# Heads 0 to 3 in the lower partitions, 4 to 7 in the upper: other pieces for the loads of a recurrence ahead of two matmul layers

## The chip, the cores and the metric

The kernel runs on one core of a Trainium2 chip. The metric is the device time of one execution in microseconds (us). PE is TensorE's matmul side, DVE is VectorE, ACT is ScalarE, POOL is GpSimd; SP issues nearly all DMA transfers of this kernel, in program order, from one queue.

## The reference, cut to what matters

```python
# attention: batch 4, heads 8, sequence 768, head size 48, fp32
for t in range(S):
    cur = einsum('bhd,bhe->bhde', u * k[t], v[t])
    y[t] = einsum('bhd,bhde->bhe', r[t], state + cur)
    state = w * state + einsum('bhd,bhe->bhde', k[t], v[t])
x = y.transpose(0, 2, 1, 3).reshape(3072, 384)
h = maximum(maximum(x @ w1, x @ w2), x @ w3); x = h @ w_out     # 384 -> 768 -> 384
g = x @ w_gate; out = (silu(g) * (x @ w_val)) @ w_out2          # 384 -> 1536 -> 384
```

## The kernel before, in words

**Units and chunks.** The sequence is cut into NB = 6 chunks of T = 128 steps. A unit is one chunk of one batch, so there are 24 units, numbered n = 4 i + b. For each unit the recurrence is done as matmuls: scores of keys against queries, masked and with a bonus on the diagonal, and a state of 48x48 per head carried from chunk to chunk. Units 0 to 3 (no state yet) are done whole at the start. From unit 4 on a unit is done in halves of 64 steps (`half`, planned as `h n`): `h n` holds the scores and state sums of unit n and the outputs y of unit n - 1.

**What a unit loads.** `load_columns` (L304, tile `qk`) brings r and reversed k with head dimension on partitions: 112 partitions by 4096 bytes that lie together, one transfer of 448 KB. `load_sides` (L325, tile `nat`, planned as `rows`) brings k, v and r with time on partitions, half the heads beside the other half, in four transfers of 144 KB. Before the change, x, the half of the partitions, holds the even or the odd heads, so that a piece of a row that lies together in memory is one head: 48 floats, 192 bytes.

**What is done with them.** DVE scales the columns by the powers of w (`prep_scores`, L342, planned as `scaled`). POOL prepares the rows (L355, L356, L360). DVE masks the scores (L405), adds up states (L515, L521) and reduces the bonus (L375). ACT copies the outputs y from PSUM into `xr` with two copies (`evacuate`, L476, planned as `row`).

**The layers between.** After a chunk's four units, two transfers (`repack`, L526, xr<-xr) bring the chunk to 128 partitions, and the first layer runs on 512 tokens: `m` (up projections, three matmul products for each pair of high and low words), a maximum over three branches on DVE (L568), its split (L580 on ACT, L583 on DVE) and `o`. Chunk 0 runs without a repack. All of this is interleaved with the units of the next chunks. The second layer (`g`, `oo`) follows from about 320 us on and has TensorE to itself.

**The weights** come in 64-bit form in 42 pieces, k = 0 to 41 (`fetch`, L226, tile `raw`, three buffers). Each is put together by ACT (L235, L242), DVE (`top` L275 and `rest` L281), ACT (L286) and POOL or DVE (`lo`, L289).

**Order.** TensorE's order is written out by hand (`order` and `slots`: `h 4` to `h 8` stand among the `m` of chunk 0). The order of the other engines and of SP's queue comes from `Plan`, a list scheduler with a cost and an earliest time for each step. Every engine runs its list in order, and so does SP: an issue that waits for a buffer holds up all later issues. `branch` (L768) tests once for decays outside a range, and what stands behind it in a list is issued after it.

Of the kernel before, what the change touches and what calls it, by code (L numbers as in the profile page):

```python
# [21 lines left out]
T = 128  # L22
# [161 lines left out]
def rwkv_moe(ctx: ExitStack, tc: tile.TileContext, qk, nat, kn, vn, rn, wcol, wh, uh, wup1, wout1, wup2, out):  # L184
# [116 lines left out]
    def load_columns(n):  # L301
        a = (h_tile([112, 2, NPAIR, T], f"qk_{n}") if n in (2, 3)
             else atp.tile([112, 2, NPAIR, T], F32, tag="qk", name=f"qk_{n}"))
        nc.sync.dma_start(out=a, in_=qk[n].rearrange("p (q j t) -> p q j t", q=2, j=NPAIR))  # L304
        inp[n] = [a]
# [9 lines left out]
    def load_sides(n):  # L315


        shape, name = [128, 2, 3, NPAIR, D], f"nat_{n}"
        if n == B:
            late["nat"] = wpool.tile([128, 2, *shape[1:]], F32, tag="w", name="nat_4_5")  # L320
        t = (late["nat"][:, n - B] if n < B + 2 else xpool.tile(shape, F32, tag=f"x2_{NB - 1}", name=name) if n == 2 * B
             else atp.tile(shape, F32, tag="nat", name=name))
        for x in range(2):
            for g in range(2):
                nc.sync.dma_start(out=t[64 * x:64 * x + 64, g].rearrange("p q j d -> p (q j) d"),  # L325
                                  in_=nat[n, 64 * g:64 * g + 64].rearrange("p (z x d) -> p x z d", x=2, d=D)[:, x])
        kvr[n] = [t[:, :, q] for q in range(3)]
        flats[n] = t.rearrange("p g q j d -> p (g q j d)")
# [4 lines left out]
    def prep_scores(n):  # L333
        a = inp[n][0]
        if n < B:
            nc.vector.tensor_tensor(out=a, in0=a, in1=powers.unsqueeze(1).to_broadcast([112, 2, NPAIR, T]), op=ALU.mult)
        else:

            halved = powers.rearrange("p j (e t) -> p j e t", e=2)[:, :, ::-1]
# [73 lines left out]
    def apply(n):  # L413
# [9 lines left out]
        for j, x, r in heads:  # L423
            h = 2 * j + x
            nc.tensor.matmul(y[r:r + D, j], v[:, h * D:(h + 1) * D], am[:, x, j], start=True, stop=True)

    def half_scores(n):
        return sc[n][:, 0].rearrange("p j (e t) -> p j e t", e=2)
# [4 lines left out]
    def half(n, before):  # L433


        works, others = [], []
        if n is not None:
            a, k, v = inp[n][0], flats[n], kvr[n][1]
            sc[n] = ps_s.tile([128, 2, NPAIR, T], F32, tag="s", name=f"s_{n}")
            for e in range(1 if n >= (NB - 1) * B else 2):  # L440
                for j in range(NPAIR):
                    for x in range(2):
                        r, c, m = 64 * x, ((1 - e) * 3 * NPAIR + j) * D, wide(x)
                        works.append((half_sums(n)[r:r + m, e, j], k[r:r + 64, c:c + m], v[r:r + 64, 1 - e, j], {}))
            for e in range(2):
                for j in range(NPAIR):
                    for x in range(2):
                        r, g = 64 * x, 64 * (1 - e)
                        works.append((half_scores(n)[r:r + 64, j, e], a[r:r + D, 1, j, g:g + 64], a[r:r + D, 0, j, 64 * e:64 * e + 64], {}))
        if before is not None:  # L450
            a, v, am = inp.pop(before)[0], kvr.pop(before)[1], ams[before]
            y = ys[before] = ps_y.tile([128, NPAIR, 2, T // 2], F32, tag="y", name=f"y_{before}")
            for e in range(2):
                s = (mids[before] if e else states[before]).rearrange("p (j d) -> p j d", j=NPAIR)
                for j in range(NPAIR):
                    for x in range(2):
                        r, to = 64 * x, y[64 - 64 * x:64 - 64 * x + D, j, e]
                        others.append((to, s[r:r + D, j], a[r:r + D, 0, j, 64 * e:64 * e + 64],
                                       dict(start=not e and not j, stop=False, skip_group_check=True)))
# [29 lines left out]
    def outer(n):  # L489
        ku, v = inp.pop(n)[1]  # L490
        ups[n] = ps_m.tile([128, NPAIR, D], F32, tag="m", name=f"u_{n}")
        kf = ku.rearrange("p h d -> p (h d)")
        for j in range(NPAIR):
            for x in range(2):
                r, h, m = 64 * x, 2 * j + x, wide(x)
                nc.tensor.matmul(ups[n][r:r + m, j], kf[:, h * D:h * D + m], v[:, h], start=True, stop=True)

# [7 lines left out]
    def decay(n, eng):  # L505
        s, m = (t.rearrange("p (j d) -> p j d", j=NPAIR) for t in (states[n], mids[n]))
        if eng is nc.scalar:
            for j in range(NPAIR):
                eng.mul(m[:, j], s[:, j], w128[0:112, j:j + 1])
            return  # L510
        eng.tensor_tensor(out=m, in0=s, in1=w128[0:112].unsqueeze(2).to_broadcast([112, NPAIR, D]), op=ALU.mult)

# [113 lines left out]
    with tc.manual_schedule():  # L626
# [49 lines left out]

        P = raw_p.tile([128, HALF], F32, tag="t", name="P")[:, 0:NPAIR * T].rearrange("p (j t) -> p j t", j=NPAIR)
        PT = tab.tile([128, H, D], F32, name="PT")
# [24 lines left out]
        square(6)  # L703
        w128 = pw[:, 7]

# [23 lines left out]
        def power_keys(eng):  # L729
            eng.tensor_tensor(  # L730
                out=P, in0=P, in1=pw[:, 6].unsqueeze(2).to_broadcast([128, NPAIR, T]), op=ALU.mult)

        def turn(_):
            pt_ps = late["pt"] = ps_y.tile([128, NPAIR, 2, 64], F32, tag="y", name="pt_ps")
            for j in range(NPAIR):
                nc.tensor.transpose(pt_ps[:, j].rearrange("p a d -> p (a d)"), P[:, j], ident)

# [95 lines left out]

        plan = Plan(dict(pe=6.4, dve=5.7, act=6.5, pool=3.3, sync=21.5, none=0.0), order)
        add = plan.add
# [73 lines left out]
        for n in range(B, NB * B):  # L909
            i, last = n // B, n >= (NB - 1) * B  # L910

            done = [("h", n - 1)] if n > B + 1 else []
            add(("load", n), {"sync": 1.3}, done or [("s", n - B)], lambda e, n=n: load_columns(n), lag=2.5,
                at=0.0 if done else 17.0 + 2 * n - 2 * B)
            space = [("rows", B)] if n == B + 1 else [("u", n - B - 2)] if n in (B + 2, B + 3) else [("h", n - 2 if n < 11 else n - 1)] if n > 2 * B else []
            if n > B:
                add(("rows", n), {"sync": 3.6}, space, lambda e, n=n: load_sides(n), lag=2.5, at=17.0 if n < 2 * B else 40.0)
# [3 lines left out]
            add(("scaled", n), {"dve": 1.35}, [("load", n), ("low", B - 1), ("lo", 1)], lambda e, n=n: prep_scores(n))  # L921
            add(("keys", n), {"pool": 1.03}, [("bonus", n), ("sided",)], lambda e, n=n: prep_keys(n))
# [12 lines left out]
            add(("row", n), {"act": 1.17}, [("h", n + 1)] + ([("xlo", i - 1, k) for k in range(NK)] if i > 1 else []),  # L935
                lambda e, n=n: evacuate(n))
# [162 lines left out]
```

## Time and profile before

| | |
|---|---|
| median of 3 runs | 832.49 us (832.34 to 834.37) |
| the profiled execution | 831.82 us, span 830.1 us |
| TensorE busy | 814.2 us (98% of the span), mean granted clock 0.995 |
| VectorE, ScalarE, GpSimd busy | 366.1, 302.9, 137.1 us |
| DMA | 83065 packets, 73.78 MB, 66520 of the packets under 512 bytes |

The span runs from the first instruction to the last; the 1.7 us between it and the execution's time lie around it. The engines' shares are averages over stages that differ: units 0 to 3 up to about 26 us, then chunk 0 of the first layer with `h 4` to `h 8` up to about 100 us, then a long stretch up to 320 us, then the second layer.

### The profile page before, as it was taken

Reading aid. Unit: us, or ns where it says so; the run is one execution under the profiler, and the core shown is the slowest. Engines: PE = TensorE matmul, PEld = TensorE weight load, DVE = VectorE, ACT = ScalarE, POOL = GpSimd, SP = SyncE. Lnnn points to the kernel's source line nnn. Section 1 sums busy time; section 2 is a strip of 40 time slices with the busy share of each in tenths; the row PEclk is TensorE's granted clock in tenths of the full one; section 3 lists DMA queues with packets and bytes.
Section 4 is the critical chain, followed back from the end, with each engine's and each line's share of the span. In section 5 each row is a group of like instructions: output and inputs, shape, how many; then the busy total and the mean of one; then the engine's idle time right before and its main releaser. Section 6 shows DMA issues by size and latency. Waiting matters only on the chain.

```text
span 830.1 us, 14338 instructions
## 1 busy us (share of the span) xinstructions
PE 814.2 (98%) x6058; PEld 672.0 (81%) x6058; DVE 366.1 (44%) x554; ACT 302.9 (36%) x579; POOL 137.1 (17%) x147
## 2 busy tenths in 40 slices
PE   9978899999999999999999999999999999999998
PEld 8766688888888888888888888888888888888886
DVE  7779866637565644234663222322222222223222
ACT  5577763425444422224672211312221122123211
POOL 5653525233342320000120000000000000000000
PEclk9989999999999999999999999999999999999999
DMA  9896954675767464311230100100010010001001
GB/s 254 200 215 175 255 131 139 145 203 142 168 198 166 112 204 177 110 65 58 87 113 1 39 0 1 39 0 1 1 39 0 1 39 0 1 1 39 0 1 38
DMA packets 83065, 73.78 MB, mean 89 GB/s; under 512 B 66520, under 2 KB 67544, under 8 KB 82232
## 3 DMA queue, kind: packets, MB, share of 16 engines
q1 hardware_dynamic: 82992, 72.86, 32.4%
q8 instruction: 47, 0.77, 0.4%
q14 instruction: 18, 0.15, 0.1%
q10 hardware_dynamic: 8, 0.00, 0.0%
HBM read 57.51 MB, written 14.16 MB: 86 GB/s over the span
## 4 chain that ended last, share of the span: by engine, by line
PE 90%; DMA 3%; DVE 2%; ACT 1%; issue 1%; SPq 0%; DVEq 0%; ACTq 0%
PE g L549 12%; PE g L551 12%; PE g L550 12%; PE m L549 8%; PE m L551 8%; PE m L550 8%; PE oo L549 6%; PE oo L551 6%; PE oo L550 6%; PE o L549 3%; PE o L550 3%; PE o L551 3%; PE s L467 2%; DMA qk<-in_qk 2%; PE y L467 2%
## 5 line engine op out<-in xcount | busy, mean ns | idle before, releaser
L549 PE MATMUL g<-xhi,w_c 128*128 128x512 f32 x432 | 168.0, 389 | 0.0
L550 PE MATMUL g<-xlo,w_c 128*128 128x512 f32 x432 | 168.0, 389 | 0.0
L551 PE MATMUL g<-xhi,w_c 128*128 128x512 f32 x432 | 168.0, 389 | 0.0
L606 DVE TENSOR_TENSOR g<-mm,g 128x512 f32<-128x512 f32 x72 | 50.1, 696 | 257.0 <-PE g L551 256.3
L549 PE MATMUL m<-xhi,w_a 128*128 128x512 f32 x324 | 129.1, 398 | 1.9 <-ACT am L384 1.7
L551 PE MATMUL m<-xhi,w_a 128*128 128x512 f32 x324 | 127.4, 393 | 2.7 <-DVE w_a L289 2.6
L550 PE MATMUL m<-xlo,w_a 128*128 128x512 f32 x324 | 127.1, 392 | 1.1 <-DVE xlo L544 0.9
L602 ACT ACTIVATE mm<-g 128x512 f32<-128x512 f32 x72 | 43.1, 599 | 151.0 <-PE g L551 151.0
L551 PEld LDWEIGHTS g<-xhi,w_c 128*128 128x128 f32 x432 | 81.1, 188 | 16.9
L550 PEld LDWEIGHTS g<-xlo,w_c 128*128 128x128 f32 x432 | 81.1, 188 | 16.8
L549 PEld LDWEIGHTS g<-xhi,w_c 128*128 128x128 f32 x432 | 81.1, 188 | 16.7
L611 ACT CAST gs<-g 128x512 fp32r<-128x512 f32 x72 | 42.3, 587 | 134.5 <-DVE g L606 134.5
L549 PE MATMUL oo<-gs,w_c 128*128 128x512 f32 x216 | 84.0, 389 | 0.0
L550 PE MATMUL oo<-gs,w_c 128*128 128x512 f32 x216 | 84.0, 389 | 0.0
L551 PE MATMUL oo<-gs,w_c 128*128 128x512 f32 x216 | 84.0, 389 | 0.0
L551 PEld LDWEIGHTS m<-xhi,w_a 128*128 128x128 f32 x324 | 61.2, 189 | 16.6 <-DVE w_a L289 3.8
L549 PEld LDWEIGHTS m<-xhi,w_a 128*128 128x128 f32 x324 | 61.1, 189 | 16.2 <-ACT am L384 1.8
L550 PEld LDWEIGHTS m<-xlo,w_a 128*128 128x128 f32 x324 | 61.1, 189 | 14.3 <-DVE xlo L544 1.8
L583 DVE TENSOR_TENSOR gs<-g,gs 128x512 fp32r<-128x512 f32 x72 | 49.8, 691 | 43.2 <-ACT gs L611 43.2
L580 ACT CAST hs<-m 128x512 fp32r<-128x512 f32 x33 | 19.3, 586 | 81.6 <-DVE m L568 81.4
L551 PEld LDWEIGHTS oo<-gs,w_c 128*128 128x128 f32 x216 | 40.6, 188 | 8.4
L550 PEld LDWEIGHTS oo<-gs,w_c 128*128 128x128 f32 x216 | 40.6, 188 | 8.4
(131 smaller groups left out, 1141.8 us busy)
## 6 DMA issues: line engine op xcount, KB each, us to landing
raw<-in_wup SPq DMA_DIRECT2D x36, 576.0 KB, 6.0
nat<-in_nat SPq DMA_DIRECT2D x80, 144.0 KB, 4.7
qk<-in_qk SPq DMA_DIRECT2D x24, 448.0 KB, 5.2
aside<-parts SPq DMA_DIRECT2D x12, 576.0 KB, 5.4
w_c<-aside SPq DMA_DIRECT2D x6, 1152.0 KB, 5.3
out<-ob SPq DMA_DIRECT2D x18, 256.0 KB, 2.1
raw<-in_wout SPq DMA_DIRECT2D x6, 384.0 KB, 4.2
y<-x SPq DMA_DIRECT2D x3, 768.0 KB, 8.3
```

The source lines that it names most:

```text
L467: nc.tensor.matmul(to, w, x, **(how or dict(start=True, stop=True)))
L549: nc.tensor.matmul(p, wh_, xh, start=first, stop=False)
L550: nc.tensor.matmul(p, wh_, xl, start=False, stop=False)
L551: nc.tensor.matmul(p, wl_, xh, start=False, stop=last)
L580: nc.scalar.copy(hsplit[i, f][0], banks["m", i, f, 2])
L583: nc.vector.tensor_tensor(out=g[1], in0=p, in1=g[0].bitcast(F32), op=ALU.subtract)
L602: nc.scalar.activation(out=hs[i, f], in_=banks["g", i, f, 0], func=AF.Silu)
L606: nc.vector.tensor_tensor(out=p, in0=hs[i, f], in1=p, op=ALU.mult)
L611: nc.scalar.copy(t[:, 0], banks["g", i, f, 1])
```

## The change

From unit 4 on, z, the half of the partitions, holds heads 0 to 3 or 4 to 7. Four heads of a row lie together in memory, so a piece of a row is 768 bytes. The columns lie in memory with even and odd heads on the halves, so they come in four transfers, and the two pairs of a tile change places (`even_first`). The outputs go back to the old order in four copies. The tables of powers are needed in both orders: `Pz` is made from `P129` with four transfers, and ACT copies it to PSUM (`powers_z`).

```diff
     def load_columns(n):
...
+        if n < B:
+            nc.sync.dma_start(out=a, in_=qk[n].rearrange("p (q j t) -> p q j t", q=2, j=NPAIR))
+        else:
+            rows = qk.rearrange("n p (q z c) -> (n p) q z c", q=2, z=2)
+            parts_ = [(z, x, 0, D if z or x and n == NB * B - 1 else 64) for z in range(2) for x in range(2)]
+            for z, x, p0, p1 in parts_ + [(0, 1, D, 64)] * (n == NB * B - 1):
+                at = 112 * n + (64 * x if p0 == 0 else 0)
+                nc.sync.dma_start(out=a[64 * z + p0:64 * z + p1, :, 2 * x:2 * x + 2].rearrange("p q j t -> p q (j t)"),
+                                  in_=rows[at + p0:at + p1, :, z])
     def load_sides(n):
...
-        for x in range(2):
+        for z in range(2):
             for g in range(2):
-                nc.sync.dma_start(out=t[64 * x:64 * x + 64, g].rearrange("p q j d -> p (q j) d"),
-                                  in_=nat[n, 64 * g:64 * g + 64].rearrange("p (z x d) -> p x z d", x=2, d=D)[:, x])
+                nc.sync.dma_start(out=t[64 * z:64 * z + 64, g].rearrange("p q j d -> p q (j d)"),
+                                  in_=nat[n, 64 * g:64 * g + 64].rearrange("p (q z c) -> p q z c", q=3, z=2)[:, :, z])
     def evacuate(n):
...
-        for r in (0, 64):
-            nc.scalar.copy(xr[i][r:r + D, :, b * T:(b + 1) * T], y[64 - r:64 - r + D])
+        for z in range(2):
+            for x in range(2):
+                nc.scalar.copy(xr[i][64 * x:64 * x + D, 2 * z:2 * z + 2, b * T:(b + 1) * T],
+                               y[64 - 64 * z:64 - 64 * z + D, 2 * x:2 * x + 2])
...
-        load_sides(B)
-        for n in range(B):
-            load_keys(n)
-        for x in range(2):
-            nc.sync.dma_start(out=ub[64 * x:64 * x + 64],
-                              in_=uh.rearrange("(j x) d -> x j d", x=2)[x:x + 1].to_broadcast([64, NPAIR, D]))
...
+        Pz = x2_space(4, [128, NPAIR, T + 1], "Pz")
+        wz = tab.tile([128, NPAIR], F32, name="wz")
+        nc.gpsimd.memset(Pz[32:64], 1.0)
...
+        nc.vector.tensor_copy(P129[:, :, T], pw[:, 7])
+        for z in range(2):
+            for x in range(2):
+                nc.sync.dma_start(out=Pz[64 * z:64 * z + D, 2 * x:2 * x + 2], in_=P129[64 * x:64 * x + D, 2 * z:2 * z + 2])
+        load_sides(B)
+        for n in range(B):
+            load_keys(n)
+        for x in range(2):
+            nc.sync.dma_start(out=ub[64 * x:64 * x + 64],
+                              in_=uh[NPAIR * x:NPAIR * x + NPAIR].unsqueeze(0).to_broadcast([64, NPAIR, D]))
...
         def power_keys(eng):
-                out=P, in0=P, in1=pw[:, 6]...
+                out=P2, in0=P, in1=pw[:, 6]...
+        def powers_z(_):
+            late["powers"] = ps_u.tile([128, NPAIR, T], F32, tag="u", name="powers_z")[0:112]
+            nc.scalar.copy(late["powers"], Pz[0:112, :, 0:T])
+            nc.scalar.copy(wz[0:112], Pz[0:112, :, T])
         def sided(_):
             for x in range(2):
-                nc.sync.dma_start(out=PT2[64 * x:64 * x + 64, x], in_=PT[64 * x:64 * x + 64, x:H:2])
-                nc.sync.dma_start(out=PT2[64 * x:64 * x + 64, 1 - x], in_=PT[64 - 64 * x:128 - 64 * x, x:H:2])
+                own = PT[:, NPAIR * x:NPAIR * x + NPAIR]
+                nc.sync.dma_start(out=PT2[64 * x:64 * x + 64, x], in_=own[64 * x:64 * x + 64])
+                nc.sync.dma_start(out=PT2[64 * x:64 * x + 64, 1 - x], in_=own[64 - 64 * x:128 - 64 * x])
...
-        plan = Plan(dict(pe=6.4, dve=5.7, act=6.5, pool=3.3, sync=21.5, none=0.0), order)
+        plan = Plan(dict(pe=6.4, dve=5.7, act=6.5, pool=3.3, sync=20.0, none=0.0), order)
-        add(("sided",), {"sync": 3.3}, [("turned",)], sided, lag=3.0)
+        add(("powers z",), {"act": 0.75}, [("scaled", B - 1)], powers_z, at=16.0)
+        add(("sided",), {"sync": 2.0}, [("turned",)], sided, lag=3.0)
-            add(("load", n), {"sync": 1.3}, ...
+            add(("load", n), {"sync": 1.9}, ...
-                add(("rows", n), {"sync": 3.6}, ...
+                add(("rows", n), {"sync": 2.4}, ...
-            add(("row", n), {"act": 1.17}, ...
+            add(("row", n), {"act": 1.56}, ...
```

The step `scaled` of units from 4 on also waits for `powers z`, and `decay` reads `wz` instead of `pw[:, 7]`. The matmuls are the same in number and size; their heads are numbered otherwise.

## Rows read from the trace of the kernel before

**Rows 1.** Stretches: length; PE, PEld, DVE, ACT, POOL busy; clock; DMA share; GB/s.
```profile
26.60:44.20 17.60, 17.49 (x181) 13.51 (x181) 10.57 (x15) 9.52 (x22) 9.54 (x9) 1.00 1.02 213
44.20:55.20 11.00, 6.66 (x138) 5.06 (x137) 10.31 (x15) 8.19 (x22) 4.46 (x3) 0.69 1.12 239
55.20:66.00 10.80, 9.01 (x162) 7.40 (x158) 8.09 (x11) 7.11 (x17) 7.93 (x8) 1.00 0.89 202
66.00:100.00 34.00, 29.76 (x360) 22.48 (x359) 32.05 (x49) 26.38 (x60) 12.75 (x12) 1.00 0.85 210
100.00:320.00 220.00, 220.00 (x2735) 182.31 (x2735) 129.91 (x203) 95.37 (x191) 74.33 (x82) 1.00 0.59 156
```

**Rows 2.** The chain of waits, 26 to 102 us: start, length, what.
```profile
35.76 8.09 DMA qk<-in_qk
...
50.90 0.43 PE m L551
...
56.17 0.23 PE m L549
...
57.18 5.94 DMA qk<-in_qk
...
75.28 5.09 DMA qk<-in_qk
...
89.76 0.58 ACT xr L476
...
92.02 4.10 DMA xr<-xr
```

**Rows 3.** The timeline of PE, 26 to 105 us, instructions that follow a wait.
```profile
45.91 0.47 PE L549 MATMUL m<-xhi,w_a 128*128 128x512 f32 x1 [1.71 <-ACT am L384]
49.25 0.80 PE L551 MATMUL m<-xhi,w_a 128*128 128x512 f32 x1 [2.64 <-DVE w_a L289]
```

**Rows 4.** The timeline of DVE, 26 to 104 us: start, length, instruction, idle time before.
```profile
43.88 1.28 DVE L342 TENSOR_TENSOR qk<-qk,powers 112x512 f32<-112x512 f32 x2 [3.32 <-DMA qk<-in_qk]
45.09 0.68 DVE L568 TENSOR_TENSOR h<-h,m 128x512 f32<-128x512 f32 x1
...
63.14 1.29 DVE L342 TENSOR_TENSOR qk<-qk,powers 112x512 f32<-112x512 f32 x2 [2.44 <-DMA qk<-in_qk]
...
80.39 1.29 DVE L342 TENSOR_TENSOR qk<-qk,powers 112x512 f32<-112x512 f32 x2 [0.83 <-DMA qk<-in_qk]
```

**Rows 5.** The timeline of SP's queue, 0 to 130 us: issues, merged where neighbours.
```profile
8.12 8.43 SPq L325 DMA_DIRECT2D nat<-in_nat  x4
...
27.95 0.34 SPq L226 DMA_DIRECT2D raw<-in_wup  x1
...
29.28 5.53 SPq L325 DMA_DIRECT2D nat<-in_nat  x4
...
51.18 5.90 SPq L325 DMA_DIRECT2D nat<-in_nat  x4
57.18 0.68 SPq L304 DMA_DIRECT2D qk<-in_qk  x1
...
117.90 2.84 SPq L325 DMA_DIRECT2D nat<-in_nat  x4
```

**Rows 6.** Stretches in which one kind of load fills the DMA engines.
```profile
12.00:15.50 3.50, 3.24 (x42) 2.74 (x42) 3.19 (x4) 1.46 (x6) 1.93 (x3) 1.00 1.03 416
16.80:19.40 2.60, 2.60 (x36) 2.23 (x34) 1.96 (x3) 2.02 (x7) 0.73 (x1) 1.00 1.44 143
20.20:22.20 2.00, 2.00 (x36) 1.69 (x34) 1.97 (x3) 2.00 (x4) 1.07 (x2) 1.00 1.02 305
```

**Rows 7.** Groups of instructions by shape: two copies on ACT.
```profile
L476 ACT COPY xr<-y 48x512 f32<-48x512 f32 x40 | 23.3, 581 | 10.2 <-PE y L467 9.1 <-DVE xlo L544 0.4
L519 ACT COPY st<-u 112x192 f32<-112x192 f32 x4 | 1.2, 313 | 0.1
```

**Rows 8.** The timeline of ACT, 14 to 27 us.
```profile
18.42 0.17 ACT L373 COPY a<-diag 128x8 f32<-128x8 f32 x1 [0.55 <-PE diag L351]
```

More of the change, by code (lines that the diff above doesn't have):

```diff
@@ L303, in load_columns @@
              else atp.tile([112, 2, NPAIR, T], F32, tag="qk", name=f"qk_{n}"))
-        nc.sync.dma_start(out=a, in_=qk[n].rearrange("p (q j t) -> p q j t", q=2, j=NPAIR))
+        if n < B:
[7 more added lines that the diff above has]
+                                  in_=rows[at + p0:at + p1, :, z])
         inp[n] = [a]
@@ L337, in prep_scores @@
         else:
-            halved = powers.rearrange("p j (e t) -> p j e t", e=2)[:, :, ::-1]
+            halved = late["powers"].rearrange("p j (e t) -> p j e t", e=2)[:, :, ::-1]
             for q in range(2):
@@ L425, in apply, with even_first @@
             nc.tensor.matmul(y[r:r + D, j], v[:, h * D:(h + 1) * D], am[:, x, j], start=True, stop=True)
+    def even_first(j):
+        return 2 * (j % 2) + j // 2
     def half_scores(n):
@@ L443, in half @@
                         r, c, m = 64 * x, ((1 - e) * 3 * NPAIR + j) * D, wide(x)
-                        works.append((half_sums(n)[r:r + m, e, j], k[r:r + 64, c:c + m], v[r:r + 64, 1 - e, j], {}))
+                        works.append((half_sums(n)[r:r + m, e, even_first(j)], k[r:r + 64, c:c + m], v[r:r + 64, 1 - e, j], {}))
             for e in range(2):
@@ L448, in half @@
                         r, g = 64 * x, 64 * (1 - e)
-                        works.append((half_scores(n)[r:r + 64, j, e], a[r:r + D, 1, j, g:g + 64], a[r:r + D, 0, j, 64 * e:64 * e + 64], {}))
+                        works.append((half_scores(n)[r:r + 64, j, e], a[r:r + D, 1, even_first(j), g:g + 64],
+                                      a[r:r + D, 0, even_first(j), 64 * e:64 * e + 64], {}))
         if before is not None:
@@ L456, in half @@
                     for x in range(2):
-                        r, to = 64 * x, y[64 - 64 * x:64 - 64 * x + D, j, e]
-                        others.append((to, s[r:r + D, j], a[r:r + D, 0, j, 64 * e:64 * e + 64],
+                        r, q = 64 * x, even_first(j)
+                        to = y[64 - r:64 - r + D, q, e]
+                        others.append((to, s[r:r + D, q], a[r:r + D, 0, q, 64 * e:64 * e + 64],
                                        dict(start=not e and not j, stop=False, skip_group_check=True)))
@@ L494, in outer @@
             for x in range(2):
-                r, h, m = 64 * x, 2 * j + x, wide(x)
-                nc.tensor.matmul(ups[n][r:r + m, j], kf[:, h * D:h * D + m], v[:, h], start=True, stop=True)
+                r, h, m = 64 * x, NPAIR * x + j, wide(x)
+                nc.tensor.matmul(ups[n][r:r + m, even_first(j)], kf[:, h * D:h * D + m], v[:, h], start=True, stop=True)
     def new_state(n):
@@ L508, in decay @@
             for j in range(NPAIR):
-                eng.mul(m[:, j], s[:, j], w128[0:112, j:j + 1])
+                eng.mul(m[:, j], s[:, j], wz[0:112, j:j + 1])
             return
-        eng.tensor_tensor(out=m, in0=s, in1=w128[0:112].unsqueeze(2).to_broadcast([112, NPAIR, D]), op=ALU.mult)
+        eng.tensor_tensor(out=m, in0=s, in1=wz[0:112].unsqueeze(2).to_broadcast([112, NPAIR, D]), op=ALU.mult)
     def middle(n):
@@ L675, in rwkv_moe @@
         off = const.tile([128, NPAIR + 1], F32, name="off")
-        P = raw_p.tile([128, HALF], F32, tag="t", name="P")[:, 0:NPAIR * T].rearrange("p (j t) -> p j t", j=NPAIR)
+        P129 = raw_p.tile([128, HALF], F32, tag="t", name="P")[:, 0:NPAIR * (T + 1)].rearrange("p (j t) -> p j t", j=NPAIR)
+        P = P129[:, :, 0:T]
+        P2 = raw_p.tile([128, HALF], F32, tag="t", name="P2")[:, 0:NPAIR * T].rearrange("p (j t) -> p j t", j=NPAIR)
+        Pz = x2_space(4, [128, NPAIR, T + 1], "Pz")
+        wz = tab.tile([128, NPAIR], F32, name="wz")
+        nc.gpsimd.memset(Pz[32:64], 1.0)
         PT = tab.tile([128, H, D], F32, name="PT")
@@ L703, in rwkv_moe @@
         square(6)
-        w128 = pw[:, 7]
+        nc.vector.tensor_copy(P129[:, :, T], pw[:, 7])
[8 more added lines that the diff above has]
+                              in_=uh[NPAIR * x:NPAIR * x + NPAIR].unsqueeze(0).to_broadcast([64, NPAIR, D]))
         powers = ps_u.tile([128, NPAIR, T], F32, tag="u", name="powers")[0:112]
@@ L730, in power_keys @@
             eng.tensor_tensor(
-                out=P, in0=P, in1=pw[:, 6].unsqueeze(2).to_broadcast([128, NPAIR, T]), op=ALU.mult)
+                out=P2, in0=P, in1=pw[:, 6].unsqueeze(2).to_broadcast([128, NPAIR, T]), op=ALU.mult)
         def turn(_):
@@ L735, in turn @@
             for j in range(NPAIR):
-                nc.tensor.transpose(pt_ps[:, j].rearrange("p a d -> p (a d)"), P[:, j], ident)
+                nc.tensor.transpose(pt_ps[:, j].rearrange("p a d -> p (a d)"), P2[:, j], ident)
+        def powers_z(_):
+            late["powers"] = ps_u.tile([128, NPAIR, T], F32, tag="u", name="powers_z")[0:112]
+            nc.scalar.copy(late["powers"], Pz[0:112, :, 0:T])
+            nc.scalar.copy(wz[0:112], Pz[0:112, :, T])
         def turned(_):
@@ L912, in rwkv_moe @@
             done = [("h", n - 1)] if n > B + 1 else []
-            add(("load", n), {"sync": 1.3}, done or [("s", n - B)], lambda e, n=n: load_columns(n), lag=2.5,
+            add(("load", n), {"sync": 1.9}, done or [("s", n - B)], lambda e, n=n: load_columns(n), lag=2.5,
                 at=0.0 if done else 17.0 + 2 * n - 2 * B)
@@ L916, in rwkv_moe @@
             if n > B:
-                add(("rows", n), {"sync": 3.6}, space, lambda e, n=n: load_sides(n), lag=2.5, at=17.0 if n < 2 * B else 40.0)
+                add(("rows", n), {"sync": 2.4}, space, lambda e, n=n: load_sides(n), lag=2.5, at=17.0 if n < 2 * B else 40.0)
             else:
@@ L920, in rwkv_moe @@
             add(("bonus", n), {"pool": 2.05}, [("rows", n), ("rest", 2)], lambda e, n=n: prep_bonus(n, engine[e]))
-            add(("scaled", n), {"dve": 1.35}, [("load", n), ("low", B - 1), ("lo", 1)], lambda e, n=n: prep_scores(n))
+            add(("scaled", n), {"dve": 1.35}, [("load", n), ("low", B - 1), ("lo", 1), ("powers z",)], lambda e, n=n: prep_scores(n))
             add(("keys", n), {"pool": 1.03}, [("bonus", n), ("sided",)], lambda e, n=n: prep_keys(n))
@@ L934, in rwkv_moe @@
             add(("select", n), {"dve": 0.7}, [("h", n), ("fill", n, 0), ("fill", n, 1)], lambda e, n=n: select(n))
-            add(("row", n), {"act": 1.17}, [("h", n + 1)] + ([("xlo", i - 1, k) for k in range(NK)] if i > 1 else []),
+            add(("row", n), {"act": 1.56}, [("h", n + 1)] + ([("xlo", i - 1, k) for k in range(NK)] if i > 1 else []),
                 lambda e, n=n: evacuate(n))
```

## The prediction

> **What bounds the kernel now.** I first read busy time in stretches, because the shares of the whole span hide the stages. From 100 to 320 us TensorE is busy 220.0 of 220.0 us, although units are loaded and evacuated there all the time [rows 1]. After that it has the second layer to itself. So nothing that the change does to loads after 100 us can shorten the run; it can only lengthen it. What is open is the stretch from 26.6 to 100 us, in which TensorE stands idle for 0.1 + 4.3 + 1.8 + 4.2 = 10.5 us (length less PE busy in the first four rows of [rows 1]).
>
> Next I read the chain of waits for that stretch. Three loads of columns stand on it, 8.09, 5.94 and 5.09 us from issue to landing, and one repack of 4.10 us [rows 2]. Then the timelines show how a late load reaches TensorE. It does so through VectorE's order: VectorE stood 3.32, 2.44 and 0.83 us before scaling the columns of three units [rows 4], and everything behind it in its list waited as well. At 43.88 us that is a maximum (45.09 us) [rows 4] and a `w_a`. TensorE's two waits at 45.91 and 49.25 us, 1.71 and 2.64 us, are these two [rows 3]. The profile names ACT for the first, but the maximum, which frees the bank, ends at 45.77, just before the matmul starts.
>
> The idle time has a second price. From 44.2 to 55.2 us the granted clock averages 0.69 [rows 1], and the step of a product's matmul is 0.43 us at 50.90, against 0.23 us at 56.17 [rows 2]: the lower level, 1.2 GHz, against 2.4 GHz. TensorE had stood idle 4.35 us just before. From 49.25 to about 53.9 us it therefore did work that takes half that time at the full level: 2.2 us lost. In all, 12.7 us are recoverable, and no more.
>
> Last I read why the loads are late, in SP's queue and the rates. The four issues of one unit's rows hold SP for 5.53 to 5.90 us in this stretch, and 8.43 at the start, against 2.84 us at 117.90 where the DMA engines are not crowded [rows 5]. The stretch that holds rows in 192-byte pieces moves 143 GB/s at a full DMA share, keys in 1536-byte pieces 305, weights in 4608-byte pieces with columns 416 [rows 6].
>
> **The change, part by part.**
>
> *Rows.* A unit has 64 x 12 x 4 = 3072 pieces of 192 bytes, and then 64 x 3 x 4 = 768 of 768 bytes; 590 KB both ways. At 143 GB/s that is 4.1 us, at 305 it is 1.9 [rows 6]. The saving lies between 0 (no faster) and 2.2 us a unit; I take 1.8, as 768 bytes are nearer to 1536 in count of pieces per byte than to 192. The Trainium skill, "DMA: Bandwidth & Descriptors" (Specifications), gives 512 bytes as the least size at line rate and names a read-modify-write below it; by that rule the saving would be the whole 2.2 us or more, and the sum would rise by about half a microsecond.
>
> *Columns.* 459 KB in 4096-byte pieces become 1024-byte pieces. Between 416 and 305 GB/s [rows 6] this costs 0 to 0.4 us of DMA time a unit; I take 0.3. On SP one issue becomes four. One issue took 0.34 us (a raw) to 0.71 us (2.84 / 4) [rows 5], so the addition is 1.0 to 2.1 us; the rows' four give back 0.7 us uncrowded (at 0.5 each) and some 3.5 us crowded. I take a net gain of about 1.5 us on SP a unit in the crowded stretch and a loss of about 1 us later, where SP has long pauses.
>
> *The load of 35.76 us.* SP starts at 27.95 us [rows 5], behind the branch. From there to the landing at 43.85 us come three raws (590 KB each), two columns, one unit's rows: 3.28 MB, and part of the next rows among them. At 0.3 us more for each columns and 1.8 less for the rows, without the next rows in between, 3.28 MB at 330 GB/s (between 305 and 416, nearer to the small pieces) take 9.9 us, and with 1.5 us to the last receipt it lands at about 39.5 us. VectorE is free at 40.56 (43.88 less 3.32) [rows 4]. So its wait of 3.32 us goes whole, and all behind it moves up by 3.3 us; TensorE's two waits shrink from 4.35 to about 1.05 us. **Gain 3.3 us.**
>
> *The clock.* TensorE stood 1.8 us at about 63 us (idle in the third row of [rows 1]) at a granted clock of 1.00. A wait of 1.05 us is shorter, so I expect no lower level. **Gain 2.2 us**; if the level still falls, 0.
>
> *The load of 57.18 us.* It may go when `h 5` has read its buffer, about 55 us (products are back at 56.17 [rows 2]), but SP was inside rows until 57.08 (51.18 + 5.90) [rows 5]. The new SP is through there at about 54, so it goes 2 us earlier and lands about 1 us faster: VectorE's 2.44 us [rows 4] goes. TensorE's 1.8 us goes with it, but from here VectorE is nearly full: 10.31 of 11.0 and 32.05 of 34.0 us busy [rows 1]. Work that moves up meets work that is already there. Of the 1.8 + 0.8 us (the third wait of [rows 4]) I count half. **Gain 1.3 us.**
>
> *The repack.* 4.10 us at 92.02 [rows 2], queued right behind a unit's rows. With 1.8 us less ahead of it and less interleaving: **gain 1.0 us**, bounds 0 to 1.8.
>
> *Outputs.* Two ACT copies of 0.581 us become four of half the columns. From 581 ns at 512 columns and 313 at 192 [rows 7] one of 256 is about 0.37 us: 1.47 against 1.16, so 0.31 us more, between nothing and 1.16 (copies that cost as much as before). Twenty units make 6 us of ACT, hidden after 100 us under TensorE's full stretch (ACT 95.37 of 220 [rows 1]). On the path stand the copies at 89.76 us [rows 2] and one such pair before them: **loss 0.6 us**.
>
> *Start.* The rows of unit 4, which held SP from 8.12 to 16.55 us [rows 5], go behind four `Pz` transfers of 48 pieces, so keys and `PT2` come earlier; TensorE does not wait for them there. ACT gets `powers z`: a copy of 512 columns, 0.58 us [rows 7], and a small one, 0.17 us [rows 8], 0.75 us. `Pz` lands behind the third raw: weights run at 416 GB/s up to 15.5 us and are through before 16.8, when rows alone run [rows 6]; 0.2 MB more put `Pz` at about 17.2 us. The pause of 0.55 us at 18.42 [rows 8] covers most of the 0.75. `t_0` now waits for the buffer that `Pz` is read from, which costs nothing if it lands by 17.15. VectorE gets one small copy, under 0.2 us. **Loss 0.3 us**, bounds 0 to 1.5.
>
> **Sum:** 3.3 + 2.2 + 1.3 + 1.0 - 0.6 - 0.3 = 6.9 us. The profiled execution took 831.82 us (span 830.1), so 824.9; the median of the runs is 0.7 us above it: **825.6 us**.
>
> **The rivals.**
>
> *Nearly all the idle time goes (821 us).* SP is through with its start by about 18 us, and the planner now counts it free at 20.0 + 2.0 instead of 21.5 + 3.3 = 24.8 us, so a raw and a column load may be put ahead of the branch, some 6 us before 27.95 [rows 5]. Then none of the DMA waits is left, and 12.7 less what VectorE's fullness costs, about 1.5, gives 11.2 us. For it: SP's idle time ahead of 27.95. Against it: VectorE's 32.05 of 34.0 us [rows 1].
>
> *VectorE takes over at once (830 us).* The first wait goes, but the matmul then waits for weights which VectorE assembles, the idle time stays above 2 us and the clock still falls. 3.3 - 0.9 = 2.4 us. For it: 10.31 of 11.0 us busy [rows 1]; against it: these 10.31 us begin only where VectorE stops waiting.
>
> *The four transfers come late (837 us).* If the landing is set by the last of four issues and not by the DMA backlog, each of three column loads on the chain [rows 2] comes up to 2.1 us later, less 0.5 that one gains from faster rows: 4.8 us, with 0.6 for the outputs 5.4. It decides where columns land behind 43.88 us, that is, where four issues and their receipts eat the 4.3 us that I count ahead. For it: SP needs four times as many issues; against it: 8.09 us to landing [rows 2] is far more than issue and receipt. The Trainium skill, "DMA: Bandwidth & Descriptors" (Rules for kernel authors), says the same of halves: two transfers to disjoint partition halves serialize, use one with 128 partitions. The trace of before has no column load in parts.
>
> *768-byte pieces are no faster (833 us).* Then only the losses of 0.9 are left. Against it: the step from 143 to 305 GB/s [rows 6].
>
> **How the numbers follow.** The forecast gets 0.50, nearly all 0.15, VectorE 0.19, late columns 0.10, no faster pieces 0.06. A measurement tells about 0.3%, 2.5 us, from no change. Faster: the first two and half of the third, 0.75. Slower: late columns and a little of the last, 0.11. Same: 0.14. The range reaches from the second case to the edge of the last: 820.5 to 832.5; the forecast's own is 823 to 828.5.
>
> **What would show it.** Right: VectorE's wait before `qk` near 44 us is gone; the granted clock stays at 1.00 from 44 to 56 us; rows hold SP for under 3 us; rows alone move over 250 GB/s; idle time of TensorE between 26.6 and 100 us is about 5 us. Wrong: a wait for `Pz` on ACT before 20 us that moves the first `m` behind 27 us; column loads that land over 6 us after their last issue; a new fall of the clock; or TensorE idle after 100 us.

## The result, and the profile after

The changed kernel takes 836.43 us (median of 12 runs, 834.87 to 839.34). The kernel before took 832.03 us beside it (12 runs, 828.86 to 834.37). The ratio is 1.0057, with a 95% interval of 1.0043 to 1.0071, so the change made the kernel 0.6% slower. The forecast of 825.6 us and its range were missed, and on the wrong side. The profiled execution of the changed kernel has a span of 834.8 us, 4.7 more than before.

The stretches answer [rows 1]. The columns are length; PE, PEld, DVE, ACT, POOL busy; clock; DMA share; GB/s:

```profile
26.60:44.20 17.60, 16.12 (x151) 12.58 (x149) 10.54 (x15) 9.03 (x21) 11.00 (x9) 1.00 0.87 228
44.20:55.20 11.00, 8.77 (x178) 6.64 (x177) 10.93 (x15) 8.65 (x22) 8.06 (x6) 0.84 1.06 238
55.20:66.00 10.80, 7.40 (x152) 6.15 (x151) 9.14 (x14) 7.83 (x18) 4.75 (x4) 1.00 0.66 171
66.00:100.00 34.00, 29.71 (x363) 23.30 (x362) 31.20 (x49) 26.85 (x64) 16.17 (x16) 1.00 0.65 200
100.00:320.00 220.00, 216.17 (x2656) 178.88 (x2655) 123.78 (x196) 104.08 (x243) 74.85 (x78) 0.99 0.51 158
```

Two things are to be seen. From 26.6 to 100 us TensorE stands idle for 1.48 + 2.23 + 3.40 + 4.29 = 11.4 us, where it was 10.5 before. The recoverable time was not recovered. After 100 us TensorE, which had been busy 220.0 of 220.0 us, is busy 216.17.

**The pause.** These are waits of PE, by what ended them (total, times, longest), and the timeline of PE at the first of them:

```profile
PE y L483 <- issue: 3.8, 1, 3.8
PE s L483 <- DVE am L415: 3.4, 1, 3.4
```

```profile
106.22 0.37 PE L483 MATMUL y<-am,nat 64*48 64x64 f32 x2 [3.83 <-issue]
106.52 0.79 PE L567 MATMUL m<-xhi,w_a 128*128 128x512 f32 x1
107.11 0.63 PE L568 MATMUL m<-xlo,w_a 128*128 128x512 f32 x1
```

TensorE stops at 102.39 us, two matmuls before the end of `h 9`, and goes on at 106.22. The releaser reads "issue": no semaphore that the profile shows is waited for. Grouped by step, PE's timelines of both kernels give this:

| | before | after |
|---|---|---|
| `h 9` begins | 101.21 | 100.32 |
| `h 9` lasts | 2.09 | 6.27 |
| the 54 matmuls of `m` behind it last | 12.52 | 13.96 |

The changed kernel is 0.9 us ahead when `h 9` begins. It then loses 4.2 us in `h 9` and 1.4 us in `m`, whose matmuls run at the lower clock until 109.7 us. 4.2 + 1.4 - 0.9 = 4.7 us, the whole difference of the spans. The stretches around the pause, in the columns of above, show what the DMA engines did:

```profile
100.00:103.00 3.00, 2.40 (x128) 1.94 (x127) 2.03 (x4) 2.04 (x5) 1.71 (x3) 1.00 1.00 374
103.00:106.00 3.00, 0.00 (x0) 0.00 (x0) 1.15 (x3) 0.00 (x0) 0.45 (x1) 1.00 0.59 182
106.00:110.00 4.00, 3.78 (x11) 2.93 (x11) 0.00 (x0) 2.54 (x6) 0.00 (x0) 0.57 0.61 178
```

They are full until 103 us. What fills them was issued by SP from 93.85 to 97.34 us, three writes of 768 KB (y<-x, in the second branch, which both kernels take) and a weight. One more queue appears in the table of DMA queues: q8, kind "instruction". For the whole execution (packets, MB, share of 16 engines), and then for the one microsecond from 103 to 104:

```profile
q8 instruction: 47, 0.77, 0.4%
...
q8 instruction: 1, 0.02, 6.0%
```

It has 47 packets of 16 KB. TensorE has 6058 matmuls and as many weight loads, 12,116 instructions, or 258 for each packet: by its size this is TensorE's own stream of instructions. The Trainium skill, "Runtime: NRT & Kernel Launch" (Instruction fetch mechanics), says blocks of 16 KiB, 256 instructions, over a DMA queue of its own, and calls the cost mostly hidden; the trace agrees on the size, and the experiments below show whether it is hidden here. An `h` uses up 256 instructions in 2.1 us. Around `h 9` one packet passes from 100.74 to 101.67 us before, and from 103.94 to 104.90 us after. The writes stand in the engines in both kernels; why the packet got through sooner before, these two traces alone do not show.

**The loads.** DVE's timeline, idle time in brackets, answers [rows 4]; SP's queue answers [rows 5]:

```profile
43.41 1.29 DVE L352 TENSOR_TENSOR qk<-qk,powers_z 112x512 f32<-112x512 f32 x2 [6.14 <-DMA qk<-in_qk]
...
61.33 1.29 DVE L352 TENSOR_TENSOR qk<-qk,powers_z 112x512 f32<-112x512 f32 x2 [1.44 <-DMA qk<-in_qk]
...
80.38 1.28 DVE L352 TENSOR_TENSOR qk<-qk,powers_z 112x512 f32<-112x512 f32 x2 [0.47 <-DMA qk<-in_qk]
```

```profile
24.64 0.52 SPq L226 DMA_DIRECT2D raw<-in_wup  x1
25.26 2.54 SPq L313 DMA_DIRECT2D qk<-in_qk  x4
31.52 0.34 SPq L226 DMA_DIRECT2D raw<-in_wup  x1
31.92 2.54 SPq L335 DMA_DIRECT2D nat<-in_nat  x4
34.59 0.51 SPq L226 DMA_DIRECT2D raw<-in_wup  x1
35.21 2.49 SPq L313 DMA_DIRECT2D qk<-in_qk  x4
```

Rows hold SP for 2.54 us instead of 5.53 here. Still the load that VectorE waits for, now issued from 35.21 to 37.70, is used at 43.41, 0.47 us earlier than before. VectorE itself was ready at 43.41 - 6.14 = 37.27 instead of 40.56, because the new order puts steps of a weight's assembly (L275, L281) behind the scaling, so the wait grew from 3.32 to 6.14 us. SP's queue shows two reasons. A weight and a column load went ahead of the branch, which SP then left late: its eight semaphore events at the branch fall at 29.5 to 31.4 us, against 27.0 to 27.8 before. They follow the landings: the last two parts of that column load land at 30.88 and 31.09 us, and events fall at 30.90 and 31.11. So SP stood in the branch until what was put ahead of it had landed. And one column load now takes SP 2.5 us in four issues of some 0.6.

### The profile page after: what moved, and what is told of

It is laid out like the page before. It is cut to its first block, busy times and chain, and to the rows that moved or that the text cites. A ratio compares the mean times of both kernels' runs of the same rounds, so it can differ in the third digit from the quotient of the medians.

```text
span 834.8 us, 14481 instructions
## 1 busy us (share of the span) xinstructions
PE 814.4 (98%) x6058; PEld 673.1 (81%) x6058; DVE 362.5 (43%) x552; ACT 314.3 (38%) x641; POOL 143.0 (17%) x146
## 3 DMA queue, kind: packets, MB, share of 16 engines
HBM read 57.51 MB, written 14.16 MB: 86 GB/s over the span
## 4 chain that ended last, share of the span: by engine, by line
PE 89%; DMA 4%; issue 3%; POOL 2%; SPq 1%; ACT 0%; DVE 0%; POOLq 0%; DVEq 0%; ACTq 0%
PE g L567 12%; PE g L569 12%; PE g L568 12%; PE m L567 8%; PE m L569 8%; PE m L568 7%; PE oo L569 6%; PE oo L567 6%; PE oo L568 6%; PE o L567 3%; PE o L569 3%; PE o L568 3%; PE s L483 2%; PE y L483 2%; DMA raw<-in_wup 1%
```

## The experiments

**First, the pause.** My theory was that TensorE waited for its own instructions, whose packet stood behind data in the DMA engines. The rivals: the pause belongs to work of `h 9` whose release the profile does not name, or it follows from any shift of the kernel by a microsecond. The first run takes the data away; the second leaves the data and shortens the stream.

```diff
 # e1_no_far: after, without the three writes; slow_input fills x2 with other bytes
-            with either.Else():
-                for y in y_far:
-                    nc.sync.dma_start(out=y, in_=x2[FAR - 1])
...
-        nc.sync.dma_start(out=x2[i], in_=y_far[i - FAR])
+        nc.sync.dma_start(out=flat_[:, 0:768], in_=nat[i, :, 0:768])
+        nc.sync.dma_start(out=flat_[:, 768:1536], in_=nat[i + 1, :, 0:768])
```

> Leaves out the three writes of 768 KB (y<-x) behind the second branch; the three later reads take the same bytes from an input, and the predicated copy ignores them, so the output stays. Theory (TensorE's 3.83 us pause at 102.39 us of the changed kernel is a fetch of its own instructions that waits behind these writes in the DMA engines): the pause goes, its lower clock too, h 9 lasts 2.1 us as before instead of 6.3, span about 830 and time about 831.5. Rival A (the pause belongs to the units' loads or to a semaphore that the profile does not show): the pause stays, time 836. Rival B (the 26 to 100 us stretch carries the loss): time 836 as well, with TensorE's idle time there unchanged.

```diff
 # e2_fewer_warm: after, filler matmuls of the start joined four to one
-            for _ in range(count):
+            for _ in range(count // 4):
+                nc.tensor.matmul(spares, ident, ident.unsqueeze(1).to_broadcast([128, 4, T]), start=True, stop=True)
+            for _ in range(count % 4):
```

> The 27 filler matmuls of 128 columns before 27 us become 7 of 512 and a few of 128, so TensorE works as long but has some 70 instructions fewer ahead of h 9; nothing else changes. Theory (instruction fetch): the place where the fetched block ends moves some 35 matmuls behind h 9, into products that use up instructions ten times slower, and the pause at 102 us goes or shrinks below 1 us although the writes y<-x are still there; time about 831.5. Rival A: the number of instructions has no bearing, the pause stays at 3.8 us, time 836.

Measured: 832.01 us without the writes (831.37 to 835.32), ratio to before 0.9989 (0.9973 to 1.0005); 832.05 us with fewer fillers (829.4 to 833.55), 0.9987 (0.9968 to 1.0007). Both lose the 4.4 us. Stretches of e1 from 100 us, and q8 from 100 to 101 us; then the same of e2, with q8 from 103 to 104:

```profile
100.00:103.00 3.00, 2.72 (x131) 2.24 (x130) 2.07 (x4) 2.06 (x6) 1.71 (x3) 1.00 0.02 5
103.00:106.00 3.00, 3.00 (x14) 2.44 (x15) 1.89 (x5) 2.47 (x6) 0.40 (x1) 1.00 0.40 123
...
q8 instruction: 1, 0.02, 7.1%
```

```profile
100.00:103.00 3.00, 3.00 (x134) 2.50 (x132) 1.63 (x3) 2.63 (x6) 1.51 (x2) 1.00 1.00 366
103.00:106.00 3.00, 3.00 (x14) 2.46 (x14) 2.42 (x6) 2.55 (x6) 1.02 (x1) 1.00 0.52 157
...
q8 instruction: 1, 0.02, 6.0%
```

Without the writes the DMA engines are empty (0.02), the packet passes at 100.24 us, 3.7 earlier, and `h 9` lasts 2.62 us. With the writes and fewer fillers the engines are as full as after and the packet passes no earlier, but TensorE has 6022 matmuls instead of 6058 (54 fillers became 18, more than the 27 of the expectation), 36 with their weight loads or 72 instructions fewer ahead of this place, and does not need it yet: `h 9` lasts 2.08 us. `h 9` began at 100.27 and 100.91 us, beside 100.32 after, so the shift is not the cause. The other profiles agree. In all six that have the pause (the changed kernel, e3, e4, e5, e7, e10) it stands ahead of the same place in TensorE's stream, its 1222nd or 1223rd matmul, and it ends 1.3 to 1.5 us after the packet has passed. The reading "issue" alone would not have told: a wait of 0.65 to 1.59 us ahead of `h 8` reads "issue" in every profile, and stays ahead of `h 8` in the shortened streams too, so it is of another kind.

Two controls put the same edits into the kernel before:

> The kernel before with the filler matmuls joined, nothing else. It is the control: if the joined fillers gain by themselves, time is 830 or less; theory: the kernel before has no pause of this kind in an h, so within 1 us of 832, minus or plus what the moved fetches do to the waits of up to 1.3 us that stand in it.

> The kernel before without the three writes y<-x, the control to the changed kernel without them, which gained 4.4 us. Theory: no fetch falls due in an h there, so the writes cost the kernel before less than 1 us; time 831 to 832. Rival (the writes hold up every kernel, by the DMA share that they take): time 828.

Measured: 831.97 us with fewer fillers (0.9998, 0.9979 to 1.0016) and 831.97 us without the writes (0.9981, 0.9964 to 0.9998). So the edits are worth 0 to 0.2% by themselves, and it is the pause that they take away from the changed kernel.

The writes are not the whole cause. In e1 the engines are empty from 98 to 100 us (share 0.01), and still the packet passes only at 100.24, as `h 9` begins; in e11, the kernel before without the writes, it begins to pass at 97.20. By this the changed kernel asked for it some 3 us later. The writes then delay it by 3.7 us in the changed kernel (103.94 instead of 100.24) and by 3.5 in the kernel before (100.74 instead of 97.20). The kernel before was just in time: its 1222nd matmul runs at 103.07 us, 1.4 behind the packet. Why the changed kernel asked later stays open.

**Second, the loads.** Two runs undo one of the two suspects each, and a third undoes both:

```diff
 # e3_one_column: after, columns laid out beforehand as the tile wants them, one transfer
...
-            for z, x, p0, p1 in parts_ + [(0, 1, D, 64)] * (n == NB * B - 1):
...
+        nc.sync.dma_start(out=a, in_=qk[n].rearrange("p (q j t) -> p q j t", q=2, j=NPAIR))
 # e4_old_plan: after, with the planner's costs of before (load 1.3, rows 3.6, row 1.17 too)
-        plan = Plan(dict(pe=6.4, dve=5.7, act=6.5, pool=3.3, sync=20.0, none=0.0), order)
+        plan = Plan(dict(pe=6.4, dve=5.7, act=6.5, pool=3.3, sync=21.5, none=0.0), order)
-        add(("sided",), {"sync": 2.0}, [("turned",)], sided, lag=3.0)
+        add(("sided",), {"sync": 3.3}, [("turned",)], sided, lag=3.0)
...
 # e5_old_plan_one_column: both
```

> Heads stay as in the change, but the columns are laid out beforehand in the new order, so that a unit's columns come in one transfer of 4096-byte pieces again. Theory (the four issues of 2.5 us in SP's queue keep the loads as late as they were): the load that landed at 43.41 us lands 2 us earlier, the next at 61.33 about 2.5 us earlier, TensorE's idle time from 26.6 to 100 us falls from 11.4 to about 7; whether the pause at 102 us stays is open, time 832 with it. Rival (VectorE or the place of the branch holds the stretch): idle time stays at 11 us, time 836.

> The changed kernel with the planner's old costs and SP's old free time, so that the order of the lists is about that of the kernel before. Theory (the load of columns that the new costs put ahead of the branch keeps SP in front of it until 27.9 us, so that fetch 4 and the rows go 2.6 us later): SP issues fetch 4 before 29.5 us, and the load that landed at 43.41 us lands at about 41; idle time of TensorE from 26.6 to 100 us falls by 2 to 3 us; the pause at 102 us may stay, time 833 to 834. Rival (the order does not matter): idle time as it is, time 836.

> The changed heads with the planner's old costs (so no load of columns ahead of the branch) and with columns in one transfer of 4096-byte pieces. Theory (each of the two alone leaves the other's delay: the branch keeps SP until 31.5 us, or the four issues of 2.5 us and the DMA backlog keep the load behind 43 us): SP reaches the load of unit 5 at about 33.3 us instead of 35.2, it lands at 40 to 41 us, VectorE's wait for it falls from 6.1 to under 2 us, TensorE's idle time from 26.6 to 100 us falls from 11.4 to about 6. The pause in h 9 may stay: 831 with it, 827 without. Rival (the DMA engines, not SP's order, hold the load): it lands at 43 us again, idle time 10 us, time 833 to 836.

Measured: 837.47 us (1.006, 1.0034 to 1.0087), 833.34 us (1.0003, 0.9984 to 1.0022) and 831.19 us (0.9989, 0.9965 to 1.0013). These are DVE's first wait in e3 and in e4, and SP's queue in e4:

```profile
43.58 1.29 DVE L342 TENSOR_TENSOR qk<-qk,powers_z 112x512 f32<-112x512 f32 x2 [6.28 <-DMA qk<-in_qk]
```

```profile
45.84 1.28 DVE L352 TENSOR_TENSOR qk<-qk,powers_z 112x512 f32<-112x512 f32 x2 [3.26 <-DMA qk<-in_qk]
```

```profile
29.23 2.56 SPq L313 DMA_DIRECT2D qk<-in_qk  x4
...
35.70 4.54 SPq L313 DMA_DIRECT2D qk<-in_qk  x4
```

Neither edit alone brings the load forward in these profiles. With one transfer SP is still late behind its branch: it takes the branch at 26.36 us, but goes on only when the column load put ahead of it has landed, at 30.43. With the old plan the four issues end at 40.24. The expectations of an earlier load were missed in both. In the medians the old plan alone gives 3.1 us back, and one transfer alone nothing. The profile of e4 is of its slowest execution (836.66 us of 831.46 to 836.66), with a pause of 3.20 us in `h 9`, so it does not show where a usual one gains. SP's queue of e5, and one of its stretches:

```profile
27.86 2.56 SPq L325 DMA_DIRECT2D nat<-in_nat  x4
30.76 0.33 SPq L226 DMA_DIRECT2D raw<-in_wup  x1
31.19 0.37 SPq L304 DMA_DIRECT2D qk<-in_qk  x1
```

```profile
44.20:55.20 11.00, 8.60 (x158) 6.79 (x156) 10.60 (x15) 8.44 (x22) 4.50 (x4) 1.00 0.77 205
```

With both undone SP's eight events fall at 25.7 to 26.3 us, the load is issued at 31.19, VectorE has no wait for it, the clock stays at 1.00, and `h 9` begins at 95.22 us, 6.0 ahead of before. That is about the gain that I had forecast, and the run lost it in the same place: `h 9` lasts 4.55 us, with a pause of 2.2 us, and the `m` behind it 14.16. So the next run adds the fewer fillers, in a version that computes all of the reference:

> The one before it with the filler matmuls joined as in the run with fewer of them, so that the fetch of instructions does not fall due in h 9; the output is the full one. Theory: the pause in h 9 is gone whatever the rest does; time 4 us under the run before it, 827. Rival: the pause only moves to another place, time as that run.

Measured: 827.25 us (825.5 to 829.43), ratio 0.9926 (0.9902 to 0.995). This is the fastest full version, and beats both kernels; its columns, like those of e3 and e5, are laid out beforehand. Its stretch after 100 us is whole again:

```profile
100.00:320.00 220.00, 220.00 (x2643) 182.12 (x2635) 128.73 (x200) 100.25 (x219) 72.18 (x80) 1.00 0.49 152
```

**Third, each part on the kernel before.** e7 takes the rows alone, in pieces of 768 bytes (heads land elsewhere, so its output is not the reference's); e9 takes the columns alone, in four transfers.

```diff
 # e7_rows_alone
-                                  in_=nat[n, 64 * g:64 * g + 64].rearrange("p (z x d) -> p x z d", x=2, d=D)[:, x])
+                                  in_=nat[n, 64 * g:64 * g + 64].rearrange("p (q z c) -> p q z c", q=3, z=2)[:, :, x])
 # e9_columns_in_four
...
+            for z in range(2):
+                for p0, p1 in ((0, 64), (64, 112)):
+                    nc.sync.dma_start(out=a[p0:p1, :, 2 * z:2 * z + 2].rearrange("p q j t -> p q (j t)"), in_=rows[p0:p1, :, z])
```

> The kernel before with nothing changed but the pieces of the rows: 768 bytes, so heads 0 to 3 land where even heads belong, and the output is not the reference's. No column transfers, no Pz, no further copies, no change of plan. Theory (the rows alone give what the prediction counted, the rest of the change takes it back): SP's four issues fall from 5.5 us to under 3.5 in the stretch, the load of unit 5 lands at 40 us, idle time falls by 3 us or more, the lower clock at 48 us goes, time 826 to 828, if the fetch of instructions does not fall due in an h. Rival (rows were not what kept the loads late): time 832, idle time 10 us.

> The kernel before with nothing changed but the columns of units from 4 on, which come in four transfers of 1024-byte pieces to where they came in one; old plan, rows in 192-byte pieces. Theory (the four transfers cost what the rows give): SP is held 2 us more for each, the loads of units 5 and 6 land 1.5 to 2.5 us later than at 43.85 and 63.12, h 9 begins 2 to 4 us later than at 101.21, time 834 to 836. Rival (the DMA backlog, not the issues, sets the landing): h 9 within 1 us, time 832.

Measured: 830.99 us for the rows (0.9984, 0.9961 to 1.0007) and 835.27 us for the columns (1.0029, 1.0011 to 1.0047). `h 9` begins at 99.20 and 105.40 us, 2.0 earlier and 4.2 later than before. DVE's waits in e9:

```profile
45.84 1.29 DVE L348 TENSOR_TENSOR qk<-qk,powers 112x512 f32<-112x512 f32 x2 [1.73 <-DMA qk<-in_qk]
...
66.38 1.28 DVE L348 TENSOR_TENSOR qk<-qk,powers 112x512 f32<-112x512 f32 x2 [5.22 <-DMA qk<-in_qk]
```

These loads are used 2.0 and 3.2 us later than the same ones in [rows 4]. The profile is of the slowest of ten executions (837.39 us), so the 4.2 us are more than the 2.4 of the ratio. The four transfers cost by themselves. In the changed kernel undoing them alone gains nothing (e3), because SP stands in the branch; with the old plan the medians differ by 2.2 us (e4 and e5), but their intervals overlap. The expectation for e7, 826 to 828 us, was missed, and its interval includes no change. In its profile the 2.0 us are spent in `h 9` again, which lasts 4.03 us there instead of 2.09.

**Last, the two that I expected to go lower.**

> Changed heads, old plan, columns in one transfer, and the three writes y<-x left out as in the run without them (the later reads take other bytes that the predicated copy ignores). Theory: h 9 begins at 95 us as in the run with old plan and one column, 6 us ahead of the kernel before, without the pause of 2.2 us and the lower clock behind it, which stood for 4.1 us there; span 824.5, time 826. Rival (without the pause the weights of the next chunk are late instead): span 827 or more.

```diff
 # e12_two_copies: e6, with heads left where the halves have them
-            for x in range(2):
-                nc.scalar.copy(xr[i][64 * x:64 * x + D, 2 * z:2 * z + 2, b * T:(b + 1) * T],
-                               y[64 - 64 * z:64 - 64 * z + D, 2 * x:2 * x + 2])
+            nc.scalar.copy(xr[i][64 * z:64 * z + D, :, b * T:(b + 1) * T], y[64 - 64 * z:64 - 64 * z + D])
```

> The best version so far (changed heads, old plan, columns in one transfer, fewer fillers) with two output copies of 48x512 in place of four of 48x256; heads end up in other rows, so the output is not the reference's. Theory: ACT saves 0.34 us a unit, of which two units stand on the path before 100 us: 0.5 us or less, time 826.8 to 827.3. Rival (the copies are what VectorE and the maxima wait for): h 9 begins over 1 us earlier, time 826 or less.

e10 is e5 without the writes; it gave 829.7 us (0.9965, 0.9944 to 0.9987). The expectation was missed. `h 9` lasts 3.16 us, so the pause has shrunk to 0.8, but in this profile it begins at 98.83, although everything ahead of it is issued from the same lists as in e5. DVE waits there:

```profile
61.33 1.29 DVE L344 TENSOR_TENSOR qk<-qk,powers_z 112x512 f32<-112x512 f32 x2 [3.33 <-DMA qk<-in_qk]
```

Two executions of such lists thus differ by over 3 us before `h 9`, and e6 and e12 show the same (98.37 and 95.42): where one profile stands alone, a difference of that size ahead of `h 9` proves little. There are no writes in e10, and its engines are empty (share 0.00) from 96 to 99 us, yet the packet passes only from 99.32 to 100.25 and TensorE stands for 0.78 us. So a packet that is asked for late suffices for a short pause. Why e10 gains less than e6 stays open.

e12 is e6 with two output copies of 48x512 instead of four of 48x256. It gave 827.18 us (0.9939, 0.9922 to 0.9956) beside 827.25 of e6: the two extra copies cost nothing that can be measured. Its `h 9` begins 3 us earlier than that of e6, which was the rival's sign, but the time that goes with it did not come. The group of ACT's copies after reads:

```profile
L493 ACT COPY xr<-y 48x256 f32<-48x256 f32 x80 | 29.3, 367 | 14.5 <-PE y L483 13.2
```

## Why the prediction was wrong

- **What bounds the kernel.** That nothing done to loads after 100 us could shorten the run, only lengthen it, held. That TensorE could be stopped there by its own instructions was in no step, and in no rival. The list of signs had "TensorE idle after 100 us", with no cause behind it. This missing term is 4.2 + 1.4 = 5.6 us in the profile; without the pause the medians of e1 and e2 are 4.4 us lower.
- **The load of 35.76 us, gain 3.3: failed.** The step took SP's list as given and put 3.28 MB at 330 GB/s. SP's list changed, because the planner's new costs moved a weight and a column load ahead of the branch. I had seen that move, but only as a rival that would gain 11.2 us. It did happen, and cost: SP had to wait in the branch for the landing of what was moved ahead, and the weight and the rows behind it went 2.6 us later (31.52 and 31.92, before 28.87 and 29.28). The rate was too high as well. Of the backlogged stretches of after, the first below is rows alone, the counterpart of the 143 GB/s in [rows 6], the second mostly columns and a weight, the third mostly rows:

```profile
16.40:19.00 2.60, 2.60 (x36) 2.23 (x34) 1.50 (x4) 2.04 (x5) 0.06 (x1) 1.00 1.09 214
...
38.50:41.00 2.50, 2.50 (x61) 2.30 (x57) 0.00 (x0) 1.89 (x8) 2.42 (x4) 1.00 1.06 289
41.00:44.00 3.00, 3.00 (x15) 2.48 (x14) 0.59 (x1) 0.00 (x0) 0.93 (x1) 1.00 1.13 250
```

- **Columns, a net gain of 1.5 us on SP a unit: failed for each load by itself.** The rows do give SP back 3 us (uncrowded 0.8 and not 0.7: 2.84 less 4 x 0.5), but the column load's last issue is 2.1 us behind its first, and VectorE needs the last. The rival "the four transfers come late" had a chance of 0.10 and a price of 837 us (832.5 + 5.4 makes 838); e9 shows its mechanism, at +0.29%. The rule of the Trainium skill that I cited with it, "DMA: Bandwidth & Descriptors" (Rules for kernel authors), one transfer over all partitions instead of two to disjoint halves, agrees with e9, whose parts are also split within the rows and have smaller pieces (1024 bytes instead of 4096). In the changed kernel it became visible only once the plan was put back (e4 beside e5: 45.84 against no wait, in one profile each).
- **The clock, gain 2.2: in part.** The level fell again, but for less time: 0.84 from 44.2 to 55.2 us instead of 0.69. In e5, where VectorE's wait is gone, it stays at 1.00. But the wait alone does not decide it: in e3, with a wait of 6.28 us, it reads 1.00, and in e12, without one, 0.84.
- **The load of 57.18 us, gain 1.3: failed.** VectorE's wait shrank from 2.44 to 1.44 us, but TensorE's idle time from 55.2 to 66 us grew from 1.79 to 3.40. It is the one wait of 3.4 us for the mask (`am`, L415) shown above: the plan now puts the scaling of unit 6 ahead of the masking of unit 5.
- **Rows: right in kind, too high in size.** From 31 to 51 us four issues hold SP for 2.54 to 4.05 us, where it was 5.02 to 7.09 before (the prediction's 5.53 to 5.90 left out the two ends). Rows alone move at 214 GB/s instead of 143, under the 250 that I had named as a sign. At 214 GB/s a unit's 590 KB take 2.8 us, so 1.4 are saved and not 1.8. The rule of the Trainium skill, "DMA: Bandwidth & Descriptors" (Specifications), that 512 bytes are the least size at line rate, does not show here, and the measurement decides: pieces of 768 bytes move at 214, and weights in [rows 6] at 416 (that stretch holds weights alone, not "with columns").
- **The repack, gain 1.0: nothing came.** It is issued at 91.18 us, before 91.26, and the idle time from 66 to 100 us is 4.29 against 4.24.
- **Outputs, loss 0.6: too high.** A copy takes 367 ns, as estimated, but e12 shows no cost of the four.
- **Start, loss 0.3: about right.** The first `m` begins at 26.41 us, before 25.93; `powers z` takes 0.59 + 0.20 us on ACT and waits for no `Pz`:

```profile
23.49 0.59 ACT L767 COPY powers_z<-Pz 112x512 f32<-112x512 f32 x1
```

In sum, of 6.9 us expected ahead of 100 us, 0.9 came, and 5.6 were lost right after. With the plan and the columns put back 6.0 us come (e5, to `h 9`), and with the pause removed too the run takes 827.25 us, near the forecast; that is another kernel than the one that was forecast, and does not make the forecast right.

## What to carry to other kernels

A long queue of bulk writes can stop an engine that waits for no data at all: where a pause reads "issue", look in the table of DMA queues at when the instruction packets pass, and test it by shortening the stream; a burst of short matmuls behind a DMA backlog is where to look first. A transfer split in four is as late as its last issue, however much faster its neighbours became. A load put ahead of a branch is not early for those behind it, if the queue must wait in the branch until it has landed. When a scheduler's costs change along with a kernel, read its new order before pricing anything, because that order is itself a part of the change.

## What the runs showed that I had not expected

- TensorE's instructions travel through the same DMA engines as data, one packet of 16 KB for each 258 instructions. In the changed kernel a packet passed 3.7 us later behind a backlog at 374 GB/s than with the engines empty (e1), and TensorE stood 3.83 us, then ran at a mean granted clock of 0.57 from 106 to 110 us. What decides when a packet is requested was not settled: with the engines empty it came at 97.20 us in e11, at 100.24 in e1 as `h 9` began, and at 99.32 in e10, 0.5 us into it.
- Some 70 instructions fewer at the start of the stream decide whether the pause occurs (836.43 against 832.05 us).
- SP goes on behind the first branch only when the loads issued ahead of it have landed: in e3 it takes the branch at 26.36 us, the load lands at 30.43, and the first event falls at 30.44.
- Four issues of a column load hold SP for 2.5 us, in crowded stretches up to 4.54, where one transfer takes 0.33 to 0.71 (the kernel before, up to 100 us).
